# Attention and two feed-forward layers in one kernel: the memory part by transposes, whole blocks, and another place for a branch

## The chip, the cores and the metric

One core of a Trainium2 chip runs the whole kernel. The metric is the device time of one execution in microseconds; the median of three runs before the change is 1127.58 us (1126.03 to 1127.97).

## The reference

Three stages follow each other on fp32 data (B = 4, H = 8, S = 576, D = 64; 2304 tokens of 512).

1. Attention with a compressive memory. For each batch and head, local causal attention and a read of a memory matrix are mixed by a gate per head:

```
a     = softmax(causal(q k^T / 8))           # 576 x 576
local = a v
q_p   = where(q > 0, q, exp(q) - 1) + 1      # phi(q)
mem   = (q_p M_prev) / (q_p . z_prev + 1e-6)
x     = g * mem + (1 - g) * local            # g = sigmoid(beta[head])
```

2. A dense layer: `x = relu(x w_in)^2 w_out`, inner width 2048.
3. Eight experts: a noisy gate picks the best two for each token, `out[token] += weight * relu(x w1[e]) w2[e]`, inner width 1024.

## The kernel before, in words

**Attention, 0 to about 235 us.** Two heads share the 128 partitions, so there are 16 pairs of a batch and two heads. A pair is cut into four units u = 0 to 3 (64 units, numbered t = 4n + u): u = 0 has the query blocks 0 and 1 (128 rows each), u = 1 block 2, u = 2 block 3, and u = 3 the last 64 rows of both heads together.

For a unit `scores` (a generator with five steps) multiplies q by k on TensorE and adds the causal mask by small matmuls (L319, L326; L348, L349 for u = 3), reduces the row extremes on VectorE (L330, L351), exponentiates on ScalarE with the row sums (L335, L353), takes reciprocals of the sums on VectorE (L339, L357) and scales P on GpSimd (L345, L359; called POOL in the profile). `transp` turns P block by block on TensorE into PSUM banks 4 and 5 (L372; L380 and L382 for u = 3); bank 4 is copied to SBUF by ScalarE (L375, L381) and bank 5 by VectorE (L377, L383). `av` multiplies by v into bank 7 (L407), and then adds the memory part in the same accumulation: a matmul whose weights are the block of `mem` and whose moving operand is the identity (L412). `put_x` copies bank 7 to the transposed activations xT with ScalarE (L93). There is one bank 7, so the next unit's `av` waits until it is read.

`phi_part` makes `mem` of a pair: exp(q) on ScalarE (L275), the minimum with 1 on VectorE (L280), max(q, 0) plus that (L281), matmuls by the gated memory and z (L287, five row blocks in two groups, the last block 64 rows), and the division (L290 to L292). Its four steps run one per unit of the pair before. Conversion of the dense layer's weights (L245 to L254) is spread over the same units.

Each engine works its queue in the order in which the program is written, and the order of a turn t of the main loop is: the first two steps of scores(t+3); the last step of scores(t+1); av(t-1) with put_x; transp(t); the fourth step of scores(t+2); the third of scores(t+3); then the steps that are due late (phi, conversion, splitting). At the begin, a list written out by hand orders the first steps of units 0 to 2 and of pair 0's phi.

**Dense layer and experts, 235 us to the end.** Each fp32 product is three matmuls of high and low parts. For experts, `Part` has ph1 (L753) and ph2 (L766) per slice fc = 0 to 7 of the inner width; ph2 of a slice runs behind ph1 of the next, and hh, hl are made by ScalarE and VectorE (L757, L758) in between. Expert 0 is done in two parts, `pa` (384 rows) and `pb_`, and parts[0] is pb_; parts[1] is expert 1. Tokens above 624 per expert go through `rare_blocks`, which stands behind a branch on a count held in SBUF; with these inputs the branch is taken past the body. The count is loaded into a register of every engine (L986) before slice 1 of parts[1], and the branch (L916, called at L990) stands before slice 2. `expert_weights` loads and splits the weights of the experts to come (L588, L589) in between. Where a body is jumped over, each engine first brings the semaphores to the counts that the body would have left (the EVENT_SEMAPHORE instructions of L916).

Of the kernel before, what the change touches and what calls it, by code (L numbers as in the profile page):

```python
# [9 lines left out]
F32 = mybir.dt.float32  # L10
# [7 lines left out]
ALU = mybir.AluOpType  # L18
# [13 lines left out]
def kernel(ctx, tc, qt, kt, vt, mt, beta, w_in, w_out,  # L32
# [23 lines left out]
    def single_banks():  # L56
# [3 lines left out]
        bank[:4] = [ps1.tile([P, 512], F32, name=f"bk{i}") for i in range(4)]  # L60
    xstack, x23, x01, xes = (ExitStack() for _ in range(4))
    xpool = xstack.enter_context(tc.tile_pool(name="xpool", bufs=1, side="right"))
# [24 lines left out]

    def put_x(hp, t0, src):
        n = src.shape[-1]
        while n:  # L90
            g, o = divmod(t0, G)
            w = min(n, G - o)
            nc.scalar.activation(xT[g][:, hp, o:o + w], src[:, :w], AF.Copy)  # L93
            src, t0, n = src[:, w:], t0 + w, n - w
# [84 lines left out]
    load(1, (qr_, kr_, vr_, mr_))  # L179

    zero = ab.tile([P, 384], F32, name="zero")
    nc.vector.memset(zero, 0.0)
# [85 lines left out]
    def phi_part(n):  # L268

        qq = qr_[n % 2][:, :S]  # L270
        e = ap2.tile([P, S], F32, name="phe", bufs=1)
        ph = ap2.tile([P, S], F32, name="phi", bufs=2)
        mg = ap2.tile([P, MW], F32, name="mg", bufs=1)
        mem[n] = ap2.tile([P, NB, P], F32, name="mem")
        nc.scalar.activation(e, qq, AF.Exp)  # L275
        nc.gpsimd.tensor_scalar(mg[:, :P], mr_[n % 2][:, :P], gtc[:, n % (H // 2):n % (H // 2) + 1], 1.0,
                                op0=ALU.mult, op1=ALU.mult)
        nc.gpsimd.tensor_copy(mg[:, P:], mr_[n % 2][:, P:])
        yield
        nc.vector.tensor_scalar_min(e, e, 1.0)  # L280
        nc.vector.scalar_tensor_tensor(ph, qq, 0.0, e, op0=ALU.max, op1=ALU.add)  # L281
        yield
        for ts in ((0, 1, 2), (3, 4)):
            k_ = len(ts)
            for i, t in enumerate(ts):
                w = min(P, S - t * P)
                nc.tensor.matmul(bank[6][:w, i * MW:(i + 1) * MW], ph[:, t * P:t * P + w], mg, start=True, stop=True)  # L287
            r = bank[6][:, :k_ * MW].rearrange("p (t c) -> p t c", c=MW)
            rd = ap2.tile([P, 3, 2], F32, name="rd")[:, :k_, :]
            nc.vector.tensor_scalar_add(rd, r[:, :, P:], 1e-6)  # L290
            nc.vector.reciprocal(rd, rd)
# [9 lines left out]
    def tiles(u):  # L301

        return [(0, P, 0), (1, 2 * P, P)] if u == 0 else [(u + 1, (u + 2) * P, 0)]

    def scores(t):
        n, u = units[t]
        h0 = 2 * (n % (H // 2))
        sp = two[t % 2]
        pb = ap3.tile([P, 2 * 512], F32, name="P", bufs=LEAD + 1)
        PB[t] = pb  # L310
# [3 lines left out]
        if u < NK - 1:  # L314
# [26 lines left out]
            for i, (qi, w, o) in enumerate(tl):  # L341
                for j in range(2):
                    x = 2 * i + j
                    v = pb[:, j * 512 + o:j * 512 + o + w]
                    nc.gpsimd.tensor_scalar(v, v, sm[:, x:x + 1], omg[:, h0 + j:h0 + j + 1], op0=ALU.mult, op1=ALU.mult)  # L345
        else:
            for c in range(2):
# [12 lines left out]
                                    op0=ALU.mult, op1=ALU.mult)  # L360

    def transp(t):
        n, u = units[t]
        pb = PB.pop(t)
        pt = ap3.tile([P, 2 * 512], F32, name="PT", bufs=2)
        PT[t] = pt
        if u < NK - 1:
            m = sum(w for _, w, _ in tiles(u))
            blocks = [(0, 0), (1, 1), (2, 2)] if u == 0 else [(c, c) for c in range(u + 2)]
            for j in range(2):  # L370
                for c, x in blocks:
                    nc.tensor.transpose(bank[4 + j][:, x * P:(x + 1) * P], pb[:, j * 512 + c * P:j * 512 + (c + 1) * P], ident)  # L372
                dst = pt[:, j * 512:j * 512 + m]
                if j == 0:
                    nc.scalar.activation(dst, bank[4][:, :m], AF.Copy)  # L375
                else:
                    nc.vector.tensor_copy(dst, bank[5][:, :m])  # L377
        else:
            for c in range(4):
                nc.tensor.transpose(bank[4][:, c * P:(c + 1) * P], pb[:, c * P:(c + 1) * P], ident)  # L380
            nc.scalar.activation(pt[:, :512], bank[4], AF.Copy)  # L381
            nc.tensor.transpose(bank[5][:TAIL, :P], pb[:, 4 * P:S], ident)  # L382
            nc.vector.tensor_copy(pt[:TAIL, 512:512 + P], bank[5][:TAIL, :P])  # L383

    def av(t):
        n, u = units[t]
        b, hp = n // (H // 2), n % (H // 2)
        vv = vr_[n % 2].rearrange("p (c j d) -> p c j d", c=NB, j=2)
        pt = PT.pop(t)
        q0 = (u + 1) * P if u else 0  # L390
        if u == 0:
            w = 2 * P
            work = [(0, P, 0, 0, w), (1, P, w, P, w)]
            rows = [(0, 0), (1, P)]
        elif u < NK - 1:
            w = P
            work = [(c, P, c * P, 0, w) for c in range(u + 2)]
            rows = [(u + 1, 0)]
        else:
            w = TAIL  # L400
            work = [(c, P, c * P, 0, w) for c in range(4)] + [(4, TAIL, 512, 0, w)]
            rows = [(u + 1, 0)]
        o = bank[7][:, :w]
        step = TAIL if u == NK - 1 else 512
        for i, (c, k_, x, a, e) in enumerate(work):
            for j in range(2):
                nc.tensor.matmul(o[j * D:(j + 1) * D, a:e], vv[:k_, c, j, :], pt[:k_, j * step + x:j * step + x + e - a],  # L407
                                 start=i == 0, stop=False, skip_group_check=True)
        for i, (qi, a) in enumerate(rows):
            k_ = min(P, w)  # L410
            for j in range(2):
                nc.tensor.matmul(o[j * D:(j + 1) * D, a:a + k_], mem[n][:k_, qi, j * D:(j + 1) * D], ident[:k_, :k_],  # L412
                                 start=False, stop=i + 1 == len(rows), skip_group_check=True)
        put_x(hp, b * S + q0, o)

# [77 lines left out]
    phi0 = phi_part(0)  # L493
    for x in (sg[0], sg[0], sg[1], sg[1], sg[0], sg[0], sg[0], sg[1], sg[2], phi0, sg[2], phi0, sg[1], sg[2]):
        next(x, None)
    run_late(-1)
    ahead_of = {}
    early = [[NU - 3, NU - 3, NU - 3, NU - 2], [NU - 2, NU - 2, NU - 1, NU - 1]]
    for t in range(NU):
# [10 lines left out]
        else:  # L510
            next(phi0)
        transp(t)
        if t + 2 in sg:
# [294 lines left out]
    for s, (g, fc) in enumerate(steps):  # L808
# [4 lines left out]
        if g == NG - 1 and fc == 0:  # L813
            x23.close()
            xe = xes.enter_context(tc.tile_pool(name="xe", bufs=1, side="right"))
            xb = [xe.tile([P, NCC, CAP - CAPA], F32R, name=f"xb{i}") for i in range(2)]
            slot = [xe.tile([P, 512], F32, name=f"es{i}") for i in range(2)]
            slot += [xT[NG - 1].rearrange("p c t -> p (c t)")[:, i * 512:(i + 1) * 512] for i in range(3)]
# [94 lines left out]

    def rare_blocks(most):

        with tc.If(most > 0):  # L916
            with tc.tile_pool(name="rp", bufs=1, side="right") as rp:
# [18 lines left out]
                for e in range(NE):  # L936
                    nb = nc.values_load(cnt[0:1, e:e + 1], min_val=0, max_val=NBLK)
                    with tc.For_i(0, nb) as i:
# [9 lines left out]
                        for fc in range(NFE):  # L948
# [4 lines left out]
                            nc.scalar.activation(hr, bank[0][:, :P], AF.Relu)  # L953
                            nc.tensor.matmul(bank[1], hr, wb, start=fc == 0, stop=fc == NFE - 1)
                        nc.vector.tensor_scalar_mul(ya, bank[1], gf[:, 1:2])
                        nc.gpsimd.indirect_dma_start(out=out, out_offset=bass.IndirectOffsetOnAxis(ap=ti[:, 0:1], axis=0),
# [26 lines left out]
    for i, pt in enumerate(parts):  # L983
        for fc in range(NFE):
            if fc == 1 and i == 1:
                most = nc.values_load(cnt[0:1, NE:NE + 1], min_val=0, max_val=NBLK)  # L986
                wslot.append(hact.rearrange("p a t -> p (a t)")[:, :512])
            if fc == 2 and i == 1:
                xes.close()
                rare_blocks(most)  # L990
                m2b = m2.enter_context(tc.tile_pool(name="m2b", bufs=1, side="right"))
                xpb = [m2b.tile([P, NCC, CAP], F32R, name=f"x2b{i}") for i in range(2)]
# [91 lines left out]
```

## Time and profile before

| | us |
|---|---|
| median of three runs | 1127.58 |
| the profiled execution | 1129.01 |
| its span, first to last instruction | 1127.3 |
| TensorE (PE) busy | 1104.0 (98%) |
| VectorE (DVE) busy | 590.6 (52%) |
| ScalarE (ACT) busy | 512.9 (45%) |
| GpSimd (POOL) busy | 240.2 (21%) |
| mean granted TensorE clock | 0.989 |

A busy share is a mean over the three stages. A matmul's time reaches from its start to its modelled end, and matmuls overlap in the pipe, so TensorE can be shown busy without being at its fastest: the starts of its weight loads (PEld) tell its real pace. A bracket at the end of a row says how long the engine stood idle before it and what released it; "issue" means that nothing in the profile explains the wait.

### The profile page before, as it was taken

Reading aid. Unit: us, or ns where it says so; the run is one execution under the profiler, and the core shown is the slowest. Engines: PE = TensorE matmul, PEld = TensorE weight load, DVE = VectorE, ACT = ScalarE, POOL = GpSimd, SP = SyncE. Lnnn points to the kernel's source line nnn. Section 1 sums busy time; section 2 is a strip of 40 time slices with the busy share of each in tenths; the row PEclk is TensorE's granted clock in tenths of the full one; section 3 lists DMA queues with packets and bytes.
Section 4 is the critical chain, followed back from the end, with each engine's and each line's share of the span. In section 5 each row is a group of like instructions: output and inputs, shape, how many; then the busy total and the mean of one; then the engine's idle time right before and its main releaser. Section 6 shows DMA issues by size and latency. Waiting matters only on the chain. (4 is left out here: it accounts for less than half of the span.)

```text
span 1127.3 us, 19033 instructions
## 1 busy us (share of the span) xinstructions
PE 1104.0 (98%) x7182; PEld 959.2 (85%) x7182; DVE 590.6 (52%) x1480; ACT 512.9 (45%) x1202; POOL 240.2 (21%) x359
## 2 busy tenths in 40 slices
PE   8999999999999999999999999799999999999996
PEld 5777777789999888898988988799999999999995
DVE  5787777669995444434347645334443444442211
ACT  5777777657665434324246534233333333331211
POOL 5556566600000022200202021102020202020202
PEclk8999999999999999999999999899999999999998
DMA  6996432034330011100125518435454444442113
GB/s 191 272 275 211 158 108 86 14 105 129 121 118 15 1 57 57 57 1 11 57 59 166 150 48 234 125 87 126 115 124 120 120 118 119 120 90 40 23 25 47
DMA packets 98280, 115.49 MB, mean 102 GB/s; under 512 B 9984, under 2 KB 67328, under 8 KB 98176
## 3 DMA queue, kind: packets, MB, share of 16 engines
q1 hardware_dynamic: 89664, 94.42, 27.8%
q0 software_dynamic: 8512, 19.74, 8.5%
q8 instruction: 59, 0.97, 0.4%
q14 instruction: 45, 0.37, 0.1%
HBM read 77.80 MB, written 36.33 MB: 101 GB/s over the span
## 5 line engine op out<-in xcount | busy, mean ns | idle before, releaser
L467 PE MATMUL bk<-xsplit,u 128*128 128x384 f32 x1152 | 219.8, 338 | 0.0
L557 PE MATMUL bk<-u,hsplit 128*128 128x512 f32 x864 | 215.2, 393 | 0.0
L766 PE MATMUL bk<-u,hsplit 128*128 128x512 f32 x802 | 213.9, 391 | 0.0
L467 PEld LDWEIGHTS bk<-xsplit,u 128*128 128x128 f32 x1152 | 202.5, 188 | 9.4 <-issue 3.1
L557 PEld LDWEIGHTS bk<-u,hsplit 128*128 128x128 f32 x864 | 160.7, 188 | 29.3
L766 PEld LDWEIGHTS bk<-u,hsplit 128*128 128x128 f32 x802 | 147.3, 188 | 27.0
L753 PE MATMUL bk<-xsplit,u 128*128 128x312 f32 (+1 forms) x864 | 137.5, 315 | 6.5 <-ACTq L916 6.5
L757 ACT ACTIVATE hsplit<-bk 128x312 fp32r<-128x312 f32 (+2 forms) x126 | 54.4, 432 | 190.1 <-PE bk L753 190.1
L753 PEld LDWEIGHTS bk<-xsplit,u 128*128 128x128 f32 x864 | 131.2, 192 | 9.3 <-ACTq L916 6.9
L688 POOL DMA_INDIRECT xs<-x,si x36 | 38.4, 1065 | 410.4 <-DVE runs L681 173.4
L478 ACT ACTIVATE hact<-bk 128x384 f32<-128x384 f32 x96 | 46.6, 485 | 141.0 <-PE bk L467 133.2
L589 DVE TENSOR_TENSOR u<-xT,u 128x512 fp32r<-128x512 f32 x89 | 60.9, 691 | 87.7 <-ACT u L588 86.9
L777 POOL DMA_INDIRECT out_dram<-xT,tk x30 | 47.5, 1584 | 278.2 <-ACT xT L774 271.5
L483 DVE TENSOR_TENSOR hact<-hact 128x384 f32<-128x384 f32 x64 | 35.7, 558 | 124.1 <-ACT hsplit L479 122.2
L588 ACT ACTIVATE u<-xT 128x512 fp32r<-128x512 f32 x89 | 55.6, 628 | 90.4 <-PE bk L766 82.3
L753 PE MATMUL bk<-x2b,u 128*128 128x312 f32 x576 | 87.7, 308 | 0.0
L345 POOL TENSOR_SCALAR P<-P,sm,omg 128x128 f32<-128x128 f32 (+3 forms) x128 | 77.3, 616 | 37.3 <-DVE rd L290 27.4
L753 PEld LDWEIGHTS bk<-x2b,u 128*128 128x128 f32 x576 | 83.3, 189 | 0.6
L758 DVE SCALAR_TENSOR_TENSOR hsplit<-bk,hsplit 128x312 fp32r<-128x312 f32 (+2 forms) x68 | 33.1, 487 | 96.6 <-ACT hsplit L757 92.9
L335 ACT ACTIVATE P<-bk,mx 128x128 f32<-128x128 f32 (+3 forms) x128 | 66.0, 528 | 12.6 <-DVE mx L330 12.3
L407 PE MATMUL bk<-PT,vr 128*64 128x128 f32 (+3 forms) x896 | 61.6, 271 | 0.4 <-ACT PT L375 0.3
L758 DVE SCALAR_TENSOR_TENSOR xsplit<-bk,hsplit 128x312 fp32r<-128x312 f32 (+1 forms) x58 | 27.7, 478 | 61.2 <-ACT hsplit L757 60.7
(186 smaller groups left out, 1465.4 us busy)
## 6 DMA issues: line engine op xcount, KB each, us to landing
xT<-in_moe_w_dram SPq DMA_DIRECT2D x89, 256.0 KB, 2.9
cst<-in_moe_w_in_dram SPq DMA_DIRECT2D x32, 256.0 KB, 2.8
cst<-in_moe_w_out_dram SPq DMA_DIRECT2D x32, 256.0 KB, 2.6
xs<-zero SPq DMA_DIRECT2D x5, 1536.0 KB
out_dram<-zero SPq DMA_DIRECT2D x4, 1472.0 KB
qr<-in_q_dram SPq DMA_DIRECT2D x16, 352.0 KB, 3.0
xr<-xs SPq DMA_DIRECT2D x7, 774.0 KB
vr<-in_v_dram SPq DMA_DIRECT2D x16, 320.0 KB, 3.8
```

What stands on the lines that cost most here:

```text
L335: nc.scalar.activation(pb[:, j * 512 + o:j * 512 + o + w], sp[:, j, o:o + w], AF.Exp, bias=mx[:, x:x + 1], scale=-1.0, accum_out=sm[:, x:x ...
L345: nc.gpsimd.tensor_scalar(v, v, sm[:, x:x + 1], omg[:, h0 + j:h0 + j + 1], op0=ALU.mult, op1=ALU.mult)
L407: nc.tensor.matmul(o[j * D:(j + 1) * D, a:e], vv[:k_, c, j, :], pt[:k_, j * step + x:j * step + x + e - a], start=i == 0, stop=False, skip ...
L467: nc.tensor.matmul(hb, l[:, sl], r, start=cc == 0 and n == 0, stop=cc == NCC - 1 and n == 2)
L557: nc.tensor.matmul(bank[y0 + t], l[:, sl], r, start=fc == 0 and n == 0, stop=fc == NFC - 1 and n == 2)
L588: nc.scalar.activation(hi, st, AF.Copy)
L589: eng.tensor_sub(lo, st, hi.bitcast(F32))
L753: nc.tensor.matmul(bank[bk][:, :n_], l[:, cs], r[:, cc, sl], start=cc == 0 and n == 0, stop=cc == NCC - 1 and n == 2)
L757: nc.scalar.activation(hh[:, sl], bank[bk][:, :n_], AF.Relu)
L758: nc.vector.scalar_tensor_tensor(hl[:, sl], bank[bk][:, :n_], 0.0, hh[:, sl].bitcast(F32), op0=ALU.max, op1=ALU.subtract)
L766: nc.tensor.matmul(bank[self.ybank + t], l[:, sl], r, start=fc == 0 and n == 0, stop=fc == NFE - 1 and n == 2)
L777: add = nc.gpsimd.indirect_dma_start(out=out, out_offset=bass.IndirectOffsetOnAxis(ap=self.tok[:n, t:t + 1], axis=0), in_=y, in_offset=Non ...
```

## The change

- In `av` the memory matmuls stay for unit 0 alone. For all later pairs `transp` turns two blocks of `mem` along with P in u = 0 and u = 1, and one in u = 3, into the free columns of banks 4 and 5; the copies to SBUF carry them, and `put_x` becomes an addition of bank 7 and that part on VectorE.
- The copy of bank 5 goes from VectorE to ScalarE for u = 2 and u = 3. PT has three buffers instead of two. P of u = 3 lives in two tiles of its own with zeros behind column 576.
- The last blocks are whole: phi's fifth block is rows 448 to 575, u = 3 turns 128 columns, and its last product runs over 128 rows.
- The minimum in phi goes ahead of the exponential and from VectorE to GpSimd.
- At the begin, transp(0) stands ahead of the main loop, the hand-written list is in another order, and for unit 0 VectorE scales one of the two heads.
- Load and branch of `rare_blocks` stand together behind the last ph2 of pb_, in slice 0 of parts[1], ahead of that slice's evacuation; the pools are closed in that order, and the rare body uses bank 2 in place of bank 1.

```diff
-    def put_x(hp, t0, src):
+    def put_x(hp, t0, src, more=None):
...
-            nc.scalar.activation(xT[g][:, hp, o:o + w], src[:, :w], AF.Copy)
+            if more is None:
+                nc.scalar.activation(xT[g][:, hp, o:o + w], src[:, :w], AF.Copy)
+            else:
+                nc.vector.tensor_add(xT[g][:, hp, o:o + w], src[:, :w], more[:, :w])
+                more = more[:, w:]
...
-        nc.scalar.activation(e, qq, AF.Exp)
+        nc.gpsimd.tensor_scalar(e, qq, 0.0, 0.0, op0=ALU.min, op1=ALU.add)
+        nc.scalar.activation(e, e, AF.Exp)
...
-        nc.vector.tensor_scalar_min(e, e, 1.0)
...
-                w = min(P, S - t * P)
-                nc.tensor.matmul(bank[6][:w, i * MW:(i + 1) * MW], ph[:, t * P:t * P + w], mg, start=True, stop=True)
+                a = min(t * P, S - P)
+                nc.tensor.matmul(bank[6][:, i * MW:(i + 1) * MW], ph[:, a:a + P], mg, start=True, stop=True)
...
+            turn = t and u < 2
+            m = sum(w for _, w, _ in tiles(u)) + (P if turn else 0)
...
+                if turn:
+                    nc.tensor.transpose(bank[4 + j][:, 3 * P:], mem[n][:, 2 * u + j, :], ident)
                 dst = pt[:, j * 512:j * 512 + m]
-                if j == 0:
-                    nc.scalar.activation(dst, bank[4][:, :m], AF.Copy)
+                if j == 0 or u == 2:
+                    nc.scalar.activation(dst, bank[4 + j][:, :m], AF.Copy)
...
-            nc.tensor.transpose(bank[5][:TAIL, :P], pb[:, 4 * P:S], ident)
-            nc.vector.tensor_copy(pt[:TAIL, 512:512 + P], bank[5][:TAIL, :P])
+            nc.tensor.transpose(bank[5][:, :P], pb[:, 4 * P:], ident)
+            nc.tensor.transpose(bank[5][:, P:2 * P], mem[n][:, NB - 1, :], ident)
+            nc.scalar.activation(pt[:, 512:512 + 2 * P], bank[5][:, :2 * P], AF.Copy)
...
-            work = [(c, P, c * P, 0, w) for c in range(4)] + [(4, TAIL, 512, 0, w)]
-            rows = [(u + 1, 0)]
+            work = [(c, P, c * P, 0, w) for c in range(NB)]
+            rows = []
...
-    for x in (sg[0], sg[0], sg[1], sg[1], sg[0], sg[0], sg[0], sg[1], sg[2], phi0, sg[2], phi0, sg[1], sg[2]):
+    for x in (sg[0], sg[0], sg[1], sg[1], sg[0], sg[0], sg[0], sg[1], sg[2], sg[1], phi0, sg[2], sg[1], phi0, sg[2]):
         next(x, None)
+    transp(0)
...
             if fc == 1 and i == 1:
-                most = nc.values_load(cnt[0:1, NE:NE + 1], min_val=0, max_val=NBLK)
+                xes.close()
...
-            if fc == 2 and i == 1:
-                xes.close()
-                rare_blocks(most)
...
             elif i:
                 parts[i - 1].ph2(NFE - 1, *prev)
+                if i == 1:
+                    xbs.close()
+                    rare_blocks()
             if fc == 0:
                 (parts[i - 1] if i else pa).evac(ytile, range(NT2 - 1))
```

## Rows read from the trace of the kernel before

**Rows 1.** One stretch: length, busy PE PEld DVE ACT POOL, clock, DMA, GB/s

```profile
40.00:240.00 200.00, 199.18 (x2085) 150.52 (x2082) 150.91 (x357) 141.24 (x425) 116.38 (x225) 1.00 0.49 152
```

**Rows 2.** Timeline of weight loads: start and length (us), line, count, [idle before]

```profile
33.50 0.47 PEld L412 LDWEIGHTS bk<-ident,mem 128*64 128x64 f32 x8
...
124.44 0.81 PEld L407 LDWEIGHTS bk<-PT,vr 128*64 128x64 f32 x20 [0.26 <-issue]
...
125.17 0.20 PEld L412 LDWEIGHTS bk<-ident,mem 64*64 64x64 f32 x4
...
125.44 0.64 PEld L372 LDWEIGHTS bk<-ident,P 128*128 128x128 f32 x6
...
130.91 0.25 PEld L412 LDWEIGHTS bk<-ident,mem 128*64 128x64 f32 x4
...
132.16 0.75 PEld L287 LDWEIGHTS bk<-mg,phi 128*128 128x128 f32 x6
...
135.94 0.61 PEld L287 LDWEIGHTS bk<-mg,phi 128*128 128x128 f32 x4
...
136.37 0.19 PEld L287 LDWEIGHTS bk<-mg,phi 128*64 128x64 f32 x2
...
136.73 0.78 PEld L348 LDWEIGHTS bk<-kr,qs 128*128 128x128 f32 x4 [0.17 <-issue]
...
154.88 0.47 PEld L412 LDWEIGHTS bk<-ident,mem 128*64 128x64 f32 x8
```

**Rows 3.** By line, 0 to 330 us: busy us, mean ns, idle, releaser

```profile
L372 PE MATMUL bk<-ident,P 128*128 128x128 f32 x320 | 45.4, 281 | 0.0
...
L377 DVE COPY PT<-bk 128x384 f32<-128x384 f32 (+1 forms) x48 | 28.7, 597 | 28.1 <-PE bk L372 27.8
...
L93 ACT ACTIVATE xT<-bk 128x128 f32<-128x128 f32 (+3 forms) x72 | 19.2, 279 | 38.5 <-PE bk L412 38.5
...
L280 DVE TENSOR_SCALAR phe<-phe 128x576 f32<-128x576 f32 x16 | 7.1, 445 | 0.0
...
L359 POOL TENSOR_SCALAR P<-P,sm,omgc 128x576 f32<-128x576 f32 x16 | 15.3, 955 | 13.1 <-DVE sm L357 13.1
...
L383 DVE COPY PT<-bk 64x128 f32<-64x128 f32 x16 | 4.4, 277 | 3.0 <-PE bk L382 3.0
```

**Rows 4.** Timeline of VectorE around u = 3

```profile
122.66 1.22 DVE L330 TENSOR_REDUCE mx<-bk 128x2 f32<-128x1024 f32 x1
```

**Rows 5.** Timeline of weight loads at the start

```profile
17.56 0.61 PEld L287 LDWEIGHTS bk<-mg,phi 128*128 128x128 f32 x4 [0.66 <-DVE mem L292]
```

**Rows 6.** Timeline of ScalarE and TensorE around the branch

```profile
712.18 0.43 ACT L757 ACTIVATE hsplit<-bk 128x312 fp32r<-128x312 f32 x1 [1.32 <-PE bk L753]
...
713.36 3.60 PE L753 MATMUL bk<-xsplit,u 128*128 128x312 f32 x24
...
716.80 3.58 PE L766 MATMUL bk<-u,hsplit 128*128 128x512 f32 x15
...
726.88 6.49 PE L753 MATMUL bk<-xsplit,u 128*128 128x312 f32 x24 [6.50 <-ACTq L916]
```

**Rows 7.** Lines L916 and L986: ns min/median/max, first to last start

```profile
L916 POOLq EVENT_SEMAPHORE  x5: 17/43/43, 717.6 to 719.0; - x5
...
L916 ACTq EVENT_SEMAPHORE  x2: 17/17/17, 726.8 to 726.9; - x2
...
L916 POOLq COMPARE_BRANCH  x1: 57/57/57, 714.9 to 714.9; - x1
...
L916 ACTq COMPARE_BRANCH  x1: 50/50/50, 722.4 to 722.4; - x1
...
L986 ACTq TENSOR_LOAD <-cnt x1: 466/466/466, 713.6 to 713.6; - x1
```

**Rows 8.** Two short stretches, columns as in rows 1

```profile
708.00:711.00 3.00, 3.00 (x24) 2.91 (x22) 1.89 (x4) 1.55 (x3) 0.00 (x0) 1.00 0.00 0
...
722.00:724.00 2.00, 0.00 (x0) 0.00 (x0) 0.69 (x1) 0.63 (x1) 0.00 (x0) 0.71 1.07 379
```

More of the change, by code (lines that the diff above doesn't have):

```diff
@@ L60, in single_banks @@
         bank[:4] = [ps1.tile([P, 512], F32, name=f"bk{i}") for i in range(4)]
-    xstack, x23, x01, xes = (ExitStack() for _ in range(4))
+    xstack, x23, x01, xes, xbs = (ExitStack() for _ in range(5))
     xpool = xstack.enter_context(tc.tile_pool(name="xpool", bufs=1, side="right"))
@@ L179 @@
     load(1, (qr_, kr_, vr_, mr_))
+    ptail = [ab.tile([P, NB * P], F32, name=f"Pt{i}") for i in range(2)]
+    for x in ptail:
+        nc.vector.memset(x[:, S:], 0.0)
     zero = ab.tile([P, 384], F32, name="zero")
@@ L308, in scores @@
         sp = two[t % 2]
-        pb = ap3.tile([P, 2 * 512], F32, name="P", bufs=LEAD + 1)
+        pb = ap3.tile([P, 2 * 512], F32, name="P", bufs=LEAD) if u < NK - 1 else ptail[n % 2]
         PB[t] = pb
@@ L344, in scores @@
                     v = pb[:, j * 512 + o:j * 512 + o + w]
-                    nc.gpsimd.tensor_scalar(v, v, sm[:, x:x + 1], omg[:, h0 + j:h0 + j + 1], op0=ALU.mult, op1=ALU.mult)
+                    (nc.gpsimd if t or j else nc.vector).tensor_scalar(v, v, sm[:, x:x + 1], omg[:, h0 + j:h0 + j + 1],
+                                                                       op0=ALU.mult, op1=ALU.mult)
         else:
@@ L360, in scores @@
                                     op0=ALU.mult, op1=ALU.mult)
+    apart = {}
     def transp(t):
@@ L364, in transp @@
         pb = PB.pop(t)
-        pt = ap3.tile([P, 2 * 512], F32, name="PT", bufs=2)
+        pt = ap3.tile([P, 2 * 512], F32, name="PT", bufs=3)
         PT[t] = pt
         if u < NK - 1:
-            m = sum(w for _, w, _ in tiles(u))
+            turn = t and u < 2
+            m = sum(w for _, w, _ in tiles(u)) + (P if turn else 0)
             blocks = [(0, 0), (1, 1), (2, 2)] if u == 0 else [(c, c) for c in range(u + 2)]
@@ L372, in transp @@
                     nc.tensor.transpose(bank[4 + j][:, x * P:(x + 1) * P], pb[:, j * 512 + c * P:j * 512 + (c + 1) * P], ident)
+                if turn:
+                    nc.tensor.transpose(bank[4 + j][:, 3 * P:], mem[n][:, 2 * u + j, :], ident)
                 dst = pt[:, j * 512:j * 512 + m]
-                if j == 0:
-                    nc.scalar.activation(dst, bank[4][:, :m], AF.Copy)
+                if j == 0 or u == 2:
+                    nc.scalar.activation(dst, bank[4 + j][:, :m], AF.Copy)
                 else:
                     nc.vector.tensor_copy(dst, bank[5][:, :m])
+            if turn:
+                apart[t] = [pt[:, (4 * j + 3) * P:(4 * j + 4) * P] for j in range(2)]
+                if u:
+                    apart[t + 1] = apart[t][1:]
         else:
@@ L381, in transp @@
             nc.scalar.activation(pt[:, :512], bank[4], AF.Copy)
-            nc.tensor.transpose(bank[5][:TAIL, :P], pb[:, 4 * P:S], ident)
-            nc.vector.tensor_copy(pt[:TAIL, 512:512 + P], bank[5][:TAIL, :P])
+            nc.tensor.transpose(bank[5][:, :P], pb[:, 4 * P:], ident)
+            nc.tensor.transpose(bank[5][:, P:2 * P], mem[n][:, NB - 1, :], ident)
+            nc.scalar.activation(pt[:, 512:512 + 2 * P], bank[5][:, :2 * P], AF.Copy)
+            apart[t] = [pt[:, 512 + 2 * P - TAIL:512 + 2 * P]]
     def av(t):
@@ L393, in av @@
             work = [(0, P, 0, 0, w), (1, P, w, P, w)]
-            rows = [(0, 0), (1, P)]
+            rows = [(0, 0), (1, P)] if not t else []
         elif u < NK - 1:
@@ L397, in av @@
             work = [(c, P, c * P, 0, w) for c in range(u + 2)]
-            rows = [(u + 1, 0)]
+            rows = []
         else:
             w = TAIL
-            work = [(c, P, c * P, 0, w) for c in range(4)] + [(4, TAIL, 512, 0, w)]
-            rows = [(u + 1, 0)]
+            work = [(c, P, c * P, 0, w) for c in range(NB)]
+            rows = []
         o = bank[7][:, :w]
@@ L407, in av @@
                 nc.tensor.matmul(o[j * D:(j + 1) * D, a:e], vv[:k_, c, j, :], pt[:k_, j * step + x:j * step + x + e - a],
-                                 start=i == 0, stop=False, skip_group_check=True)
+                                 start=i == 0, stop=i + 1 == len(work) and not rows, skip_group_check=True)
         for i, (qi, a) in enumerate(rows):
@@ L411, in av @@
             for j in range(2):
-                nc.tensor.matmul(o[j * D:(j + 1) * D, a:a + k_], mem[n][:k_, qi, j * D:(j + 1) * D], ident[:k_, :k_],
+                nc.tensor.matmul(o[j * D:(j + 1) * D, a:a + k_], mem[n][:, qi, j * D:(j + 1) * D], ident[:, P - k_:],
                                  start=False, stop=i + 1 == len(rows), skip_group_check=True)
-        put_x(hp, b * S + q0, o)
+        if rows:
+            put_x(hp, b * S + q0, o)
+        else:
+            for i, more in enumerate(apart.pop(t)[:len(tiles(u)) if u < NK - 1 else 1]):
+                put_x(hp, b * S + q0 + i * P, o[:, i * P:min(w, (i + 1) * P)], more)
     NU = len(units)
@@ L511 @@
             next(phi0)
-        transp(t)
+        if t:
+            transp(t)
         if t + 2 in sg:
@@ L815 @@
             xe = xes.enter_context(tc.tile_pool(name="xe", bufs=1, side="right"))
+            slot = [xe.tile([P, 512], F32, name=f"es{i}") for i in range(2)]
+            xe = xbs.enter_context(tc.tile_pool(name="xeb", bufs=1, side="right"))
             xb = [xe.tile([P, NCC, CAP - CAPA], F32R, name=f"xb{i}") for i in range(2)]
-            slot = [xe.tile([P, 512], F32, name=f"es{i}") for i in range(2)]
             slot += [xT[NG - 1].rearrange("p c t -> p (c t)")[:, i * 512:(i + 1) * 512] for i in range(3)]
@@ L912, in counts, with rare_blocks @@
             nc.vector.tensor_copy(cnt, nbf)
-    def rare_blocks(most):
+    def rare_blocks():
+        most = nc.values_load(cnt[0:1, NE:NE + 1], min_val=0, max_val=NBLK)
         with tc.If(most > 0):
@@ L953, in rare_blocks @@
                             nc.scalar.activation(hr, bank[0][:, :P], AF.Relu)
-                            nc.tensor.matmul(bank[1], hr, wb, start=fc == 0, stop=fc == NFE - 1)
-                        nc.vector.tensor_scalar_mul(ya, bank[1], gf[:, 1:2])
+                            nc.tensor.matmul(bank[2], hr, wb, start=fc == 0, stop=fc == NFE - 1)
+                        nc.vector.tensor_scalar_mul(ya, bank[2], gf[:, 1:2])
                         nc.gpsimd.indirect_dma_start(out=out, out_offset=bass.IndirectOffsetOnAxis(ap=ti[:, 0:1], axis=0),
```

## The prediction

> **What bounds the kernel now.** I read the busy times by stretch first, then the timeline of the weight loads, then the groups by line, then the branch.
>
> Attention is bound by TensorE's own stream. From 40 to 240 us TensorE has work for 199.18 of 200 us at the full clock of 2.4 GHz, VectorE for 150.91, ScalarE for 141.24, GpSimd for 116.38 [rows 1]. A busy TensorE proves little, but the pace does: the group of eight memory matmuls that opens each pair's second turn starts at 33.50 us and at 154.88 us, nine pairs apart, 13.487 us per pair [rows 2], and I found that step the same to 0.01 us for each of the nine. A chain of waits among four engines, with weight conversion coming and going, would not keep step like that. So each 0.1 us that leaves TensorE's stream in a pair is worth 1.5 us in 15 pairs, as long as no other engine comes late.
>
> Afterwards the experts run on TensorE without gaps but for one: the branch. TensorE ends a ph2 at 720.38 (716.80 + 3.58) and stands until 726.88, released by ScalarE's semaphore instruction of L916. The 24 matmuls behind take 6.49 us; the same 24 a slice earlier take 3.44 (713.36 to 716.80) [rows 6]. The granted clock has fallen from 2.4 to 1.2 GHz meanwhile: 722 to 724 us has a mean of 0.71, so it fell at 722.8, some 2.4 us after TensorE stopped [rows 8]. The branch costs 6.50 + 3.05 = 9.55 us.
>
> **The change part by part.**
>
> *Memory matmuls out.* Eight in u = 0 hold the weight path for 0.47 us, four in u = 1 or u = 2 for 0.25, so four more cost 0.22 [rows 2]: 0.44 + 0.22 + 0.22 = 0.88 us per pair. The gap behind them is the change from one tile shape to another and stays. In u = 3 from the first of four small ones to the transposes are 0.27 us (125.17 to 125.44), gap included; with the last block whole, a change from 128 to 64 rows inside `av` goes as well. I take 0.20, between 0.05 and 0.27.
>
> *phi's last block whole.* Its four matmuls and the gap behind take 0.79 us (135.94 to 136.73); the last two wait until 136.37 because their tile is 64 columns wide, and L348 waits again. Six of one shape take 0.75 with 0.19 for the last, so 0.112 apart [rows 2]: four would need 0.45. That is 0.34 less if both gaps close, 0 if they stay; I take 0.30.
>
> *Transposes in.* Five per pair. Six take 0.64 us [rows 2], 0.107 each: 0.535 us. Their length of 281 ns [rows 3] is latency in the pipe. If each cost that instead, it would be 1.40 us. The Trainium skill ("TensorE: Matmul & The Clock Gate", Part 4: PE-mode transpose) gives some 275 ns for a 128x128 transpose inside a kernel. By that figure five would cost 1.38 us and the gain in attention would be nil; the row agrees with the length, and the 0.64 us for six speak against it as a price. The 64 columns of u = 3 that become 128 cost at most one pitch more.
>
> *Sum for TensorE:* 0.88 + 0.20 + 0.30 - 0.535 = 0.85 us per pair; 13.49 becomes 12.64. Pair 0's u = 0 is left out of it; in the last pairs the splitting of x and the first dense matmuls share the engines. I count 13 of 16 pairs: 11.0 us. Bounds: nothing, if another engine takes over, to 15 (0.99 in 15 pairs).
>
> *VectorE.* It loses the minimum (0.445), one copy of 0.597 and one of 0.277; it gains five additions, which I price as the copy of 128 columns out of a bank, 0.277 each, 1.39 in all, and two copies a third wider, at most 0.2 each [rows 3]. Net +0.3 to +0.5 us per pair. Its load is 150.91/200 x 13.49 = 10.2 us now, then some 10.6 of 12.64, 84%. An addition waits in VectorE's queue for `av`; behind it stands the copy of bank 5, which waits for the transposes anyway (27.8 us in 48 copies, 0.58 each [rows 3]), so the wait is covered. The tight place is u = 3: the long reduction there runs from 122.66 to 123.88 [rows 4], the addition of u = 2 would stand behind it until about 124.16, and TensorE wants bank 7 at 124.44 [rows 2], some 0.25 earlier with the matmuls gone. That alone would miss by nothing or by a tenth. But minimum and copy (together 1.04) leave VectorE's queue ahead of that reduction and one addition comes, so it starts up to 0.7 us earlier. I cost this at nothing; without that cover 0.1 to 0.3 us per pair. VectorE is late next.
>
> *ScalarE* gives 72 copies of 0.279 away [rows 3], 1.26 us per pair, and takes two from VectorE and two wider ones: no change within 0.2. It no longer waits for `av` (38.5 us idle before those copies). *GpSimd* gains the minimum, near the 0.955 of the scaling of 576 columns [rows 3]; 7.8 of 13.49 becomes 8.8 of 12.64. ScalarE's exponential waits for it, and behind that the copies of the next turn; the minimum is issued after a unit's scaling while GpSimd stands idle, so nothing. The third PT buffer, P's own tiles for u = 3 and their zeros at the start cost nothing: the reuse distance of the others stays four units.
>
> *The begin.* transp(0) goes from behind phi's first three blocks to ahead of them. It filled part of the wait for the division, which now leaves TensorE idle longer than the 0.66 us before L287 at 17.56 [rows 5]; on the other side scaling split over two engines lets it start earlier, in a time that was empty. Between -1 and +1 us; I take 0, since both are one queue in another order.
>
> *The branch.* In the new place the last thing that ScalarE does ahead of it is L757 at 712.18, as TensorE nears its end. Loading the count takes 0.47 us, so the branch is at 712.7. From the branch to the first instruction behind GpSimd needed 2.7 us (714.9 to 717.6), ScalarE 4.4 (722.4 to 726.8) [rows 7]; the latter beside full DMA queues, while 708 to 711 has a DMA share of 0.00 [rows 8]. So ScalarE opens the way at 715.4, at worst 717.1; TensorE comes at 713.4, where the next slice's matmuls began [rows 6]. Idle 2.0 to 3.7 us; I take 2.2, nearer to the quiet row. In the old place ScalarE came to the branch at 722.4, two us after TensorE had stopped; in the new one it is there before TensorE. Load and branch without a slice between them expose the 0.47, which is counted. Whether the clock falls is open: before, it stood at 2.4 GHz through the first 2.4 us of the stop; I forecast a shorter stop and that it stays. Gain 9.55 - 2.2 = 7.3; bounds 9.55 - (2.0) = 7.5 and 9.55 - (3.7 + 3.05) = 2.8. Moved behind it are the evacuation of pb_ (two copies, and two scatters on GpSimd's queue), the last weights of expert 2 and SP's first loads for expert 3: all some 2 us later. Banks 5 and 6 are wanted by the next ph2, 3.4 us of ph1 later, when two copies of a bank are long done; the weights are for the next experts. That costs nothing.
>
> *Sum:* 11.0 + 7.3 = 18.3. The profiled execution took 1129.01 us, so 1110.7; it lies 1.4 above the median of the runs, from which the sum gives 1109.3. I say 1110.5.
>
> **The rivals.**
>
> A. *The clock falls in the new place too.* For: 2.2 us idle is close to 2.4. Against: it is shorter. Half speed until the clock is back costs up to the 3.05 seen: 1110.5 + 3 = 1113.5.
>
> B. *VectorE takes part of attention's gain* (bank 7 freed 0.3 us late in each pair, or the gaps around short tiles stay). For: 84% load in order. Against: the constant step shows slack now. Half of 11 us is lost: 1116.
>
> C. *Transposes cost their length, not their pitch:* 1.40 instead of 0.535 us, gain in attention nil, 1121.5. The pitch in rows 2 speaks against it. The page cited above would have it so.
>
> D. *Slower.* VectorE's addition sits behind reductions in every unit, and TensorE waits at bank 7 each time. The gain of 18.3 us is eaten at 18.3/63 = 0.29 us per unit; half a reduction of 1.22 in each, 0.6 us, makes 38 us: 1110.5 + 38, about 1148. For: one bank 7, strict order. Against: copies waited 0.58 us for TensorE, so VectorE is ahead of it in most units.
>
> E. *The branch costs what it did* (4.4 us of fetching plus the clock, or another engine late): attention alone, 1118.
>
> **How the numbers follow.** Forecast 0.45, A 0.25, B 0.15, C 0.04, D 0.05, E 0.05, and 0.01 that gains and new waits cancel near no change. The forecast's own range is 1107 to 1113. The range goes down to 1105 (15.0 and 7.5 us, the best bounds of both, from 1129.01 would be 1106.5, from the median 1105.1) and up to 1119, over A, B and E; C, D and the case of no change stay outside. About 0.2%, 2.3 us, is what a measurement of this kernel can tell from none: faster 0.94 (forecast, A, B, C, E), same 0.01, slower 0.05 (D).
>
> **What would show it.** The group that opens `av`'s second turn should return every 12.6 us (12.5 to 12.9), without waits of weight loads on VectorE. If 13.0 or more with releaser VectorE, B or D; with transposes 0.2 us apart, C; if the gaps before L348 and inside phi's four remain, the whole block was worth nothing. At the branch one idle of 2 to 3 us released by ScalarE, the next 24 matmuls in 3.4 us (forecast) or up to 6.5 (A), and no gap two slices later. GpSimd's minimum should have no waiter but ScalarE. The forecast is wrong if attention's end moves by less than 8 us or the branch gives less than 5.

## The result and the profile after

| | before | after |
|---|---|---|
| median, 5 runs each, one chip (us) | 1127.58 | 1117.88 |
| the profiled execution / its span (us) | 1129.01 / 1127.3 | 1117.88 / 1116.2 |
| ScalarE busy (us) | 512.9 | 510.5 |
| GpSimd busy (us) | 240.2 | 275.7 |

The ratio is 0.9918, 95% interval 0.9898 to 0.9938: 9.2 us faster where 17.1 was forecast, and inside the range. Two things are to be explained: which parts came as priced, and where the other 8 us are. The parts below are read from one profiled execution of each kernel; their spans differ by 11.1 us.

**The branch came as priced.** TensorE after, from 709 us on (start and length in us, in brackets the idle time ahead and its releaser):

```profile
709.86 0.39 PE L793 MATMUL bk<-u,xsplit 128*128 128x512 f32 x1
712.25 3.70 PE L780 MATMUL bk<-xsplit,u 128*128 128x312 f32 x24 [2.01 <-ACTq L945]
715.79 3.58 PE L793 MATMUL bk<-u,hsplit 128*128 128x512 f32 x15
```

And the stretch behind it (columns as in rows 1):

```profile
714.00:718.00 4.00, 4.00 (x24) 3.63 (x23) 2.06 (x4) 0.95 (x3) 2.35 (x2) 1.00 0.68 116
```

6.50 us of idle time [rows 6] have become 2.01, and the clock, which had fallen to 1.2 GHz [rows 8], stays at 2.4 GHz: the 24 matmuls take 715.79 - 712.25 = 3.54 us, not 6.49. 9.55 - 2.01 - (3.54 - 3.44) = 7.4 us (forecast 7.3). The branch of the sequencers of TensorE's weight loads and of ScalarE (ns min/median/max, first to last start):

```profile
L945 PEldq EVENT_SEMAPHORE  x2: 51/51/51, 711.7 to 711.9; - x2
L945 ACTq EVENT_SEMAPHORE  x2: 17/17/17, 712.2 to 712.3; - x2
L945 ACTq COMPARE_BRANCH  x1: 50/50/50, 709.4 to 709.4; - x1
```

ScalarE is at the branch at 709.4, before TensorE stops at 710.24, and opens the way 2.8 us later; 2.7 was taken, from GpSimd's row. TensorE's own sequencer was through at 711.9, so of the 2.01 us ScalarE adds some 0.3.

**TensorE's stream came as priced, the pace nearly.** Weight loads of one steady pair after:

```profile
123.93 0.63 PEld L428 LDWEIGHTS bk<-PT,vr 128*64 128x64 f32 x8 [0.21 <-issue]
124.73 0.31 PEld L385 LDWEIGHTS bk<-ident,P 128*128 128x128 f32 x3 [0.17 <-issue]
125.01 0.14 PEld L387 LDWEIGHTS bk<-ident,mem 128*128 128x128 f32 x1
125.12 0.36 PEld L385 LDWEIGHTS bk<-ident,P 128*128 128x128 f32 x3
...
132.01 0.53 PEld L296 LDWEIGHTS bk<-mg,phi 128*128 128x128 f32 x4
132.46 0.79 PEld L358 LDWEIGHTS bk<-kr,qs 128*128 128x128 f32 x4
133.30 0.10 PEld L359 LDWEIGHTS <-identb 128*128 128x128 bf16 x1
133.75 0.69 PEld L428 LDWEIGHTS bk<-PT,vr 128*64 128x64 f32 x20 [0.35 <-issue]
134.51 0.31 PEld L385 LDWEIGHTS bk<-ident,P 128*128 128x128 f32 x3
...
135.70 0.52 PEld L328 LDWEIGHTS bk<-kr,qs 64*128 64x128 f32 x8 [0.34 <-ACT qs L275]
136.25 0.32 PEld L335 LDWEIGHTS <-idh 64*128 64x128 bf16 x4
136.78 0.20 PEld L428 LDWEIGHTS bk<-PT,vr 128*64 128x64 f32 x4 [0.21 <-issue]
```

A transpose of `mem` takes 125.12 - 125.01 = 0.11 us of the stream, the four phi matmuls 132.46 - 132.01 = 0.45 instead of 0.79 [rows 2], and u = 3 goes from `av` straight to the transposes. The pair's first `av` returns after 136.78 - 123.93 = 12.85 us, against 13.49 before: 0.64 less, not 0.85. The same two places in the kernel before:

```profile
124.08 0.10 PEld L349 LDWEIGHTS <-identb 128*128 128x128 bf16 x1
...
126.24 0.52 PEld L319 LDWEIGHTS bk<-kr,qs 64*128 64x128 f32 x8 [0.17 <-ACT xT L93]
```

Two waits make the rest: the next pair's scores wait 0.34 for the scaled queries of ScalarE, where the gap before was 0.17, and from L359 to `av` of u = 3 pass 133.75 - 133.30 = 0.45 where it was 0.36 (124.08 to 124.44). Together 0.26; phi and u = 3 gave some 0.05 more than was priced.

**The minimum did not.** ScalarE and GpSimd, 0 to 245 us by line and form (busy us, mean ns, idle before, releaser), and behind them one place in the late pairs:

```profile
L284 POOL TENSOR_SCALAR phe<-qr 128x576 f32<-128x576 f32 x16 | 34.4, 2149 | 1.3
...
L285 ACT ACTIVATE phe<-phe 128x576 f32<-128x576 f32 x16 | 10.9, 684 | 20.6 <-POOL phe L284 20.6
```

```profile
194.03 2.14 POOL L284 TENSOR_SCALAR phe<-qr 128x576 f32<-128x576 f32 x1
...
196.21 0.68 ACT L285 ACTIVATE phe<-phe 128x576 f32<-128x576 f32 x1 [3.31 <-POOL phe L284]
...
196.80 0.58 ACT L390 ACTIVATE PT<-bk 128x512 f32<-128x512 f32 x1
...
197.43 0.63 PEld L428 LDWEIGHTS bk<-PT,vr 128*64 128x64 f32 x12 [2.00 <-ACT PT L390]
```

One minimum, with the addition of zero in the same instruction, takes 2.15 us on GpSimd, not 0.955. ScalarE stands 20.6 us in front of its exponentials, and what is queued behind one (here the copy of PT) reaches TensorE as an idle 2 us. The clock fell behind this one; the stretch after it:

```profile
200.00:204.00 4.00, 4.00 (x31) 2.54 (x31) 2.78 (x8) 1.45 (x5) 1.79 (x5) 0.71 0.00 0
```

At the begin the same wait delays phi's first matmuls and with them pair 0. The first `av` of pairs 0 and 10, after:

```profile
21.13 0.74 PEld L428 LDWEIGHTS bk<-PT,vr 128*64 128x64 f32 x8 [0.41 <-issue]
...
149.62 0.63 PEld L428 LDWEIGHTS bk<-PT,vr 128*64 128x64 f32 x8 [0.21 <-issue]
```

and before:

```profile
19.42 0.63 PEld L407 LDWEIGHTS bk<-PT,vr 128*64 128x64 f32 x8 [0.21 <-issue]
...
154.29 0.63 PEld L407 LDWEIGHTS bk<-PT,vr 128*64 128x64 f32 x8 [0.21 <-ACT P L353]
```

Pair 15's starts at

```profile
220.84 0.19 PEld L428 LDWEIGHTS bk<-PT,vr 128*64 128x64 f32 x2 [0.55 <-ACT PT L390]
```

where before it was

```profile
222.61 0.62 PEld L407 LDWEIGHTS bk<-PT,vr 128*64 128x64 f32 x6 [0.55 <-ACT PT L375]
```

so of 11.0 us forecast for attention 1.8 had arrived by then. At the begin 1.7 us are lost. From pair 0 to pair 10, 154.29 - 19.42 before against 149.62 - 21.13 after, 6.4 are gained. From pair 10 to pair 15, 68.32 against 71.22, 2.9 are lost. The branch adds 7.4, and 1.4 more come in the last turns and in the dense layer: TensorE's last matmul ends 10.6 us earlier.

### The profile page after: what moved, and what is told of

It reads as the page before. It is cut to its first block, busy times and chain, and to the rows that moved or that the text cites. A ratio compares the mean times of both kernels' runs of the same rounds, so it can differ in the third digit from the quotient of the medians.

```text
span 1116.2 us, 18641 instructions
## 1 busy us (share of the span) xinstructions
PE 1089.9 (98%) x6948; PEld 949.7 (85%) x6948; DVE 586.2 (53%) x1522; ACT 510.5 (46%) x1163; POOL 275.7 (25%) x373
## 5 line engine op out<-in xcount | busy, mean ns | idle before, releaser
L780 PE MATMUL bk<-xsplit,u 128*128 128x312 f32 (+1 forms) x864 | 134.7, 311 | 2.0 <-ACTq L945 2.0
L428 PE MATMUL bk<-PT,vr 128*64 128x128 f32 (+2 forms) x896 | 60.2, 269 | 6.1 <-ACT PT L390 4.1
L428 PEld LDWEIGHTS bk<-PT,vr 128*64 128x64 f32 x896 | 43.3, 137 | 21.6 <-issue 9.6
```

The lines of the kernel that those rows point to most:

```text
L780: nc.tensor.matmul(bank[bk][:, :n_], l[:, cs], r[:, cc, sl], start=cc == 0 and n == 0, stop=cc == NCC - 1 and n == 2)
```

## The experiments

Times are medians; ratios are to the kernel before on the same chip, with 95% intervals. The experiments ran on three chips, on which the median of the kernel before was 1126.91, 1125.39 and 1127.97 us, so ratios are to be compared, not times. The pairs are followed by the start of each pair's first `av` (the group of eight weight loads at L428), as above.

**1. The minimum back on VectorE.**

```
-  nc.gpsimd.tensor_scalar(e, qq, 0.0, 0.0, op0=ALU.min, op1=ALU.add)
-  nc.scalar.activation(e, e, AF.Exp)
+  nc.scalar.activation(e, qq, AF.Exp)
...
   yield
+  nc.vector.tensor_scalar_min(e, e, 1.0)
```

> The changed kernel with phi's minimum back on VectorE, behind the exponential; all else as changed. Theory W (GpSimd's minimum takes 2.14 us instead of 0.955, and ScalarE's exponential waits for it at the head of ScalarE's queue, with the PT copies and exponentials behind it): pair 0's second attention group begins about 1.5 us earlier, the steady period falls from 12.84 to about 12.65 us, the late pairs with the splitting of x lose 3 to 4 us less; 1109 to 1112 us, near the 1110.5 forecast. Rival V (VectorE's additions or the splitting of x hold the pairs back): VectorE now has 0.45 us more per pair and the time stays at 1117 or rises to 1120.

1112.67 us, 0.9871 (0.9854 to 0.9887), clear of the changed kernel's 0.9898 to 0.9938; the time is 0.7 us above W's range. W holds, V falls: pair 0 starts at 18.75 us (2.4 earlier), and the last five pairs take 66.76 us, 4.5 less than in the changed kernel and 1.6 less than before. The copy of PT at the place shown above no longer waits for an exponential:

```profile
191.59 0.60 ACT L390 ACTIVATE PT<-bk 128x512 f32<-128x512 f32 x1 [0.77 <-PE bk L387]
```

and the clock stays at 2.4 GHz through the late pairs (columns as in rows 1):

```profile
148.00:220.00 72.00, 69.96 (x680) 51.61 (x680) 54.97 (x149) 49.84 (x140) 49.49 (x93) 1.00 0.22 70
```

One number of W missed: the steady period is 12.90, not 12.65. VectorE's 0.459 us per minimum is now in the pair, and the wait for the scaled queries is still there (experiment 5).

**2. The branch alone, in the kernel before** (the load of the count, pools and bank go with it).

```
             if fc == 2 and i == 1:
-                rare_blocks(most)
...
                 parts[i - 1].ph2(NFE - 1, *prev)
+                if i == 1:
+                    rare_blocks()
```

> The kernel before with the branch alone moved (its banks, pools and the load of the count with it). Theory: the idle time of TensorE at the branch falls from 6.5 to about 2 us and the clock does not fall, so the gain is that of the whole change's trace, 7.5 us: 1120 us. Rival (the branch's gain hangs on the shorter attention, or is given back by the weights that come 2 us later): 1124 to 1127.5 us. Attention's period stays at 13.49 us in both.

1121.0 us, 0.9944 (0.9926 to 0.9962): 6.3 us, with 7.4 inside the interval. TensorE at the branch in this kernel:

```profile
715.59 2.70 PE L753 MATMUL bk<-xsplit,u 128*128 128x312 f32 x17 [1.76 <-ACTq L918]
```

The gain doesn't hang on a shorter attention.

**3. phi's whole last block alone, in the kernel before** (with the memory matmuls of u = 3 over all rows).

```
-                w = min(P, S - t * P)
-                nc.tensor.matmul(bank[6][:w, ...], ph[:, t * P:t * P + w], mg, ...)
+                a = min(t * P, S - P)
+                nc.tensor.matmul(bank[6][:, ...], ph[:, a:a + P], mg, ...)
...
-                nc.tensor.matmul(o[...], mem[n][:k_, qi, ...], ident[:k_, :k_], ...)
+                nc.tensor.matmul(o[...], mem[n][:, qi, ...], ident[:, P - k_:], ...)
```

> The kernel before with phi's last block whole alone (and the memory matmuls of the last turn over all 128 rows). Theory: the gap inside the four phi matmuls closes, 0.34 us less in some 15 pairs, 5 us: about 1122.5 us, period 13.15. Rival (TensorE only reaches another engine's wait earlier, so the time saved turns into waiting): 1127 us, period 13.4 to 13.5.

1125.66 us, 0.999 (0.998 to 1.0): the rival's number nearly, though not by its cause alone. The four matmuls do take 0.45 instead of 0.79 us, but the period falls only from 13.49 to 13.38. Weight loads of this kernel from there on:

```profile
134.58 0.53 PEld L287 LDWEIGHTS bk<-mg,phi 128*128 128x128 f32 x4
135.03 0.79 PEld L348 LDWEIGHTS bk<-kr,qs 128*128 128x128 f32 x4
...
136.23 0.81 PEld L407 LDWEIGHTS bk<-PT,vr 128*64 128x64 f32 x20 [0.26 <-issue]
137.11 0.20 PEld L412 LDWEIGHTS bk<-ident,mem 128*64 128x64 f32 x4
137.37 0.64 PEld L372 LDWEIGHTS bk<-ident,P 128*128 128x128 f32 x6
138.26 0.52 PEld L319 LDWEIGHTS bk<-kr,qs 64*128 64x128 f32 x8 [0.24 <-ACT qs L266]
```

0.34 us leave the stream and 0.24 come back, in two places. From `av` of u = 3 to its memory matmuls pass 0.88 us, where it was 0.73 (124.44 to 125.17 in rows 2). That is no wait for another engine but the experiment's own second edit: the last four loads of `av` have 64 rows in both kernels, and the memory matmuls behind them now have 128 rows (L412: 128*64 here, 64*64 in rows 2). In the kernel before they follow 0.12 us after the first of the four, here 0.26, with a new change of shape between them. This kernel, then the same place before:

```profile
136.85 0.19 PEld L407 LDWEIGHTS bk<-PT,vr 64*64 64x64 f32 x4
137.11 0.20 PEld L412 LDWEIGHTS bk<-ident,mem 128*64 128x64 f32 x4
```

```profile
138.54 0.20 PEld L407 LDWEIGHTS bk<-PT,vr 64*64 64x64 f32 x4
138.66 0.20 PEld L412 LDWEIGHTS bk<-ident,mem 64*64 64x64 f32 x4
```

The other 0.09 is a wait: the scores behind the six transposes come after 0.89, where it was 0.80, released by the scaled queries. So this run doesn't show what phi's whole block alone is worth; without the 0.15 the period would be some 13.23 (an estimate). In the changed kernel these memory matmuls are gone, and with them that gap.

**4. The minimum still on GpSimd, a turn ahead of its exponential.**

```
         nc.gpsimd.tensor_scalar(e, qq, 0.0, 0.0, op0=ALU.min, op1=ALU.add)
+        yield
         nc.scalar.activation(e, e, AF.Exp)
...
         gen = phi_part(m)
+        later(NK * (m - 1) - 1, gen)
...
     phi0 = phi_part(0)
+    next(phi0)
```

> The changed kernel with phi's minimum still on GpSimd, issued one turn ahead of its exponential. Theory W (the wait in ScalarE's queue is what costs, not GpSimd's load): most of what the minimum on VectorE would give back, 1110 to 1113 us, and the idle time of ScalarE in front of the exponential gone in the steady pairs. Rival G (GpSimd's 2.14 us themselves make the scaling of P late): the time stays at 1116 to 1119 us, with the waits now in front of the transposes or P's copies.

1114.39 us, 0.9893 (0.9876 to 0.9911), between W's range and G's. By the traces the wait in ScalarE's queue is most of it: pair 0 starts at 18.09 us, the last five pairs take 67.92, and pair 15 starts 4.3 us earlier than in the changed kernel, where experiment 1 gave 5.3. By the times it is about half (0.9918 to 0.9893, against 0.9871), and the interval overlaps that of the changed kernel. No idle time is left in front of the exponential (by line and form):

```profile
L286 ACT ACTIVATE phe<-phe 128x576 f32<-128x576 f32 x16 | 11.0, 688 | 0.0
```

G holds in part: the steady period rises to 13.00, with 0.59 us from L360 (L359 of the changed kernel) to `av` of u = 3, and among the waits of 60 to 140 us (us, times, longest) stands a new one in that turn:

```profile
ACT P L345 <- POOL phe L284: 3.9, 6, 0.6
```

**5. The scaled queries a turn earlier** (with experiment 1).

```
-        later(NK * (m - 1) - 1, first(m))
+        later(NK * (m - 1) - 2, first(m))
```

> The minimum back on VectorE, and the scaled queries of the next pair issued on ScalarE one turn earlier, into the 1.68 us in which ScalarE stands before the last turn's copy. Theory Q (of the 0.2 us per pair by which the steady period misses 12.64, 0.17 is the wait of the next pair's first scores for these queries, which stand behind two exponentials in ScalarE's queue): the step behind the last transposes falls from 0.48 to 0.31 us, the period from 12.90 to about 12.73, some 2.5 us in 15 pairs: 1110 us. Rival (TensorE only comes earlier to the copies of P, which are then late): the period stays at 12.9 and the time at 1112.7 us.

1111.8 us, 0.9871 (0.9855 to 0.9888). The period is 12.72, as Q says, and the wait is gone:

```profile
133.44 0.52 PEld L328 LDWEIGHTS bk<-kr,qs 64*128 64x128 f32 x8 [0.17 <-issue]
```

But the times can't be told from experiment 1's: the ratio is the same 0.9871, and Q's 1110 us didn't come. Pair 15 starts at 214.06 us, 1.5 earlier than in experiment 1, and yet both profiled spans are 1110.6. In this execution the 1.5 us are lost at the branch, where it met the prediction's rival A. TensorE at the branch, then the stretch behind it:

```profile
705.32 4.03 PE L780 MATMUL bk<-xsplit,u 128*128 128x312 f32 x17 [1.86 <-ACTq L945]
```

```profile
706.00:708.00 2.00, 2.00 (x11) 2.00 (x10) 1.59 (x3) 1.14 (x3) 1.55 (x1) 0.56 0.02 8
```

and the stretch behind the branch in experiment 1:

```profile
707.00:709.00 2.00, 2.00 (x15) 2.00 (x15) 0.96 (x2) 1.75 (x4) 1.12 (x1) 1.00 0.03 8
```

An idle time of 1.86 us was followed by a clock of 1.2 GHz, one of 1.83 (experiment 1) or of 2.01 (after) was not. In the profiles of experiments 6 and 7 the idle time is 1.87 in both, and the clock fell in 7 alone. What decides it these runs don't show.

**6 and 7. What makes GpSimd's instruction long.** In 7 the minimum is left out of the computation; place and waits stay.

```
-  nc.gpsimd.tensor_scalar(e, qq, 0.0, 0.0, op0=ALU.min, op1=ALU.add)
6: nc.gpsimd.tensor_scalar_min(e, qq, 0.0)
7: nc.gpsimd.tensor_scalar(e, qq, 1.0, 1.0, op0=ALU.mult, op1=ALU.mult)
```

> The changed kernel with the minimum on GpSimd as an instruction of one operation, without the addition of zero behind it. If the second operation makes the 2.14 us: about 1.0 us each, and 1112 to 1114 us. If the minimum itself is slow on GpSimd: still about 2.1 us each and 1117 to 1118 us.

> The changed kernel with GpSimd's instruction as two multiplications by 1 in place of the minimum and the addition: the minimum is left out of the computation, the instruction, its place and its waits stay. If the 2.14 us come from the operation: 0.95 to 1.2 us each, as the scalings of 576 columns, and the time is what the prediction priced, 1112 to 1114 us. If they come from the place (its tiles, or VectorE beside it): still about 2.1 us and 1117 to 1118 us.

6 is 1115.23 us, 0.991 (0.9893 to 0.9926), which by the time can't be told from the changed kernel; 7 is 1109.17 us, 0.9847 (0.983 to 0.9863). Neither instruction has the length that was expected: 6 lies between its two answers, and 7 is shorter than the 0.95 to 1.2 us of the scalings. The instruction in 6, then in 7 (by line and form):

```profile
L284 POOL TENSOR_SCALAR phe<-qr 128x576 f32<-128x576 f32 x16 | 26.5, 1657 | 1.3
```

```profile
L284 POOL TENSOR_SCALAR phe<-qr 128x576 f32<-128x576 f32 x16 | 10.9, 679 | 1.3
```

The minimum alone takes 1.66 of the 2.15 us, and two multiplications in the same place and on the same tiles take 0.68, so it is the operation that is slow. Attention follows that price in the profiled executions:

| | instruction (us) | first `av`, pair 0 | pairs 10 to 15 (us) | ratio |
|---|---|---|---|---|
| 7: multiplications | 0.68 | 19.39 | 65.43 | 0.9847 |
| 6: minimum alone | 1.66 | 20.32 | 68.68 | 0.991 |
| after: minimum, addition | 2.15 | 21.13 | 71.22 | 0.9918 |

The steady period of 7 is 12.67 us, against 12.64 forecast, and its ratio makes 1110.3 of 1127.58 us, against 1110.5. But 0.68 is less than the 0.955 that was assumed. Between the rows of 7 and 6, 0.28 us more are worth some 0.9 us in the last five pairs and 0.3 at the begin; with the price as assumed the forecast would have been missed by about 1 us (an estimate from this table).

**8. The begin in the old order** (with experiment 1).

```
-    for x in (..., sg[2], sg[1], phi0, sg[2], sg[1], phi0, sg[2]):
+    for x in (..., sg[2], phi0, sg[2], phi0, sg[1], sg[2]):
...
-    transp(0)
     run_late(-1)
...
-        if t:
-            transp(t)
+        transp(t)
```

> The minimum back on VectorE, and the begin in the order of the kernel before (phi's first step ahead of the third unit's scaling, the first transposes behind phi's first three blocks). If the order of the begin is worth nothing, as the prediction took it: within 1 us of the 1112.7 us of the kernel with the minimum on VectorE, and the first pair's second attention group at 18.7 to 19.4 us. If it costs or gives more than 1 us, this start moves by as much.

1112.23 us, 0.9884 (0.9867 to 0.99): the same as experiment 1 within the intervals. Pair 0 starts at 17.67 us, 1.1 earlier than there and earlier than expected, which the times don't show. Single traces can't settle it either, since this start differs between executions with the same begin: 17.67 here and 19.12 in experiment 10, 18.75 in experiment 1 and 19.45 in experiment 9.

**9. The branch in its old place** (experiment 1 without the branch's move).

```
                 parts[i - 1].ph2(NFE - 1, *prev)
-                if i == 1:
-                    rare_blocks()
...
+            if fc == 2 and i == 1:
+                rare_blocks(most)
```

> The minimum back on VectorE, and the branch back in its old place: the attention part of the change alone. If the parts add up, the branch's move is worth here what it was worth alone (0.56% of the time, 5.9 us at the medians, 7.8 by the two profiled spans): 1118 to 1120 us, TensorE idle 5.5 to 6.5 us at the branch with a fall of the clock behind it. If part of the branch's gain came only with the shorter attention: 1121 us and above, or 1115 and below if it hardly counts.

1119.7 us, 0.9933 (0.9916 to 0.9949): attention alone, with the minimum on VectorE, is worth 7.6 us, and the branch on top of it 0.9933 - 0.9871, 7.0 us (6.3 alone in experiment 2). Within the intervals the parts add up. TensorE at the branch, and the stretch in which the clock falls:

```profile
718.91 3.49 PE L780 MATMUL bk<-xsplit,u 128*128 128x312 f32 x12 [6.21 <-ACTq L944]
```

```profile
715.00:717.00 2.00, 0.00 (x0) 0.00 (x0) 0.69 (x1) 0.03 (x1) 0.00 (x0) 0.71 1.01 328
```

**10. Experiments 1, 5 and 8 together.**

```
-        later(NK * (m - 1) - 1, first(m))
+        later(NK * (m - 1) - 2, first(m))
...
+        nc.vector.tensor_scalar_min(e, e, 1.0)
...
+    for x in (..., sg[2], phi0, sg[2], phi0, sg[1], sg[2]):
...
-    transp(0)
...
-        if t:
-            transp(t)
+        transp(t)
```

> The version that the runs point to: the minimum on VectorE, the scaled queries a turn earlier, the begin in the order of before. Expected: the period of 12.72 us and the begin of the run with the old order together, 1110.5 to 1111.8 us. If the pairs only reach their data or the splitting of x earlier, as the run with the earlier queries alone did: 1112 us, no better than the minimum on VectorE alone.

1111.57 us, 0.986 (0.9841 to 0.9879). Better than the changed kernel, whose interval lies wholly above, but not to be told from experiment 1. The period is 12.73; pair 15 starts at 214.71 us.

## Why the prediction was right and where it was not

- *Direction and range:* right. The likeliest value was 7.4 us too low, and by its own test ("attention's end moves by less than 8 us") attention was wrong: by the branch it is 3.3 us ahead (TensorE's last matmul there starts at 709.86, before at 713.13). No rival names the cause, so that the time lies in the range is in part luck: the range was made wide for A, B and E.
- *The mis-sized term:* "GpSimd gains the minimum, near the 0.955 of the scaling of 576 columns", from which "so nothing" followed. It took 2.15 us, and ScalarE's queue, which the prediction saw waiting, did not absorb it. At 0.68 (experiment 7) the forecast's sum is met. The nearest row was of the right engine and size but of another operation, and no upper end was set. The Trainium skill ("GPSIMD Engine Reference", 4.1 Engine selection) calls GpSimd roughly line-rate for elementwise work with one input, and names VectorE as the engine to use: multiplications at 0.68 us, half as long again as VectorE's 0.459 for its minimum, come near that; the minimum at 1.66 does not.
- *The begin*, priced at 0: 1.7 us lost. In the five traces with the minimum on VectorE (experiments 1, 5, 8, 9, 10) pair 0 starts at 17.67 to 19.45 us, with it a turn ahead at 18.09 (experiment 4), and behind its wait at 20.32 and 21.13 (experiment 6, after), so the loss is the minimum's wait; the order itself is worth nothing that a time shows (experiment 8).
- *TensorE's stream:* right in each step: transposes of `mem` at their pitch of 0.11 us (C falls), phi 0.34, memory matmuls, the switch in u = 3. These are read from the stream; apart from phi's block no run takes one of them alone. But 0.26 us came back as waits. The forecast looked for them on VectorE; 0.17 was ScalarE (gone in experiment 5), whose queue holds the scaled queries behind two exponentials and, new, two copies of PT in one turn. The constant step of 13.49 us had been read as slack of the other engines; in this turn ScalarE was only 0.1 to 0.2 us behind TensorE. Where the other 0.09 comes from is not shown.
- *VectorE costs nothing:* right. In the steady pairs no weight load is released by its additions, and 0.46 us more of it per pair (experiment 1) left the period within 0.06. D falls. B's 1116 us is near what was measured, but not by B's cause. The prediction's terms for VectorE add up to +0.1 to +0.5 us, not +0.3 to +0.5, which changes nothing.
- *Thirteen of 16 pairs:* about right. By the start of pair 15 experiment 7 had 222.61 - 213.23 = 9.4 us of the 11.0, and by the branch 713.13 - 702.29 = 10.8; the changed kernel had 1.8 and 3.3.
- *The branch:* right, 7.4 for 7.3 by the trace; by times 6.3 alone and 7.0 as the last step. Rival A did come, in two other profiled executions, with idle times no longer than here (experiments 5 and 7). E falls.

## What to carry to other kernels

Price an elementwise instruction by a row of the same operation on the same engine: the row of another operation that was used here was short by a factor of 2.2 (0.955 for 2.15 us), and on the same tile the two operations differ by a factor of three (0.68 and 2.15). An instruction moved to a slower engine ahead of its reader is paid in the reader's queue, so ask what stands behind the reader, above all where that queue feeds TensorE. Of the time of matmuls cut from a stream, part can come back in the same turn: as a wait for an engine that was just behind (the scaled queries), or as a new change of shape next to the cut (experiment 3).

## What the runs showed that was not expected

- On GpSimd, 128x576 fp32 in one instruction: two multiplications by constants 0.68 us, by two per-row values 0.955 [rows 3], one minimum 1.66, minimum and addition 2.15.
- At the branch, idle times of 1.86 and 1.87 us (experiments 5 and 7) were followed by a fall of TensorE's clock from 2.4 to 1.2 GHz, and idle times of 1.87 and 2.01 (experiment 6, after) were not. A fall cost 1.5 us there: the 24 matmuls show 5.24 us, not 3.70.
